# The opening of a fused attention and SwiGLU kernel: first layer norm by tiles, dummy matmuls, an early table load and a weight load in pieces

## Chip, cores, metric

The kernel runs on one core of one Trainium2 chip. The metric is the device time of the whole program in microseconds (us), lower is better. The kernel before took 1697.18 us (median of 3 runs, 1696.16 to 1697.53).

## The reference, cut

Two layers, each a local dilated attention followed by a gated feed-forward, both behind a layer norm. The weights are the same in both layers.

```python
def _layernorm(x, axis=-1, eps=1e-5): ...           # no scale, no shift
# x: (1, 2048, 1024) bf16
x = x + A(_layernorm(x), wqkv, wo)    # 32 heads of 32; each token sees 8 keys, 2 apart
x = x + B(_layernorm(x), w1, w3, w2)  # silu(x@w1) * (x@w3) @ w2, inner width 3584
x = x + A(_layernorm(x), wqkv, wo)
x = x + B(_layernorm(x), w1, w3, w2)
```

## The kernel before

Tokens are worked on in four chunks of 512. A chunk passes a Q stage (layer norm, transposes, QKV matmuls on TensorE, stores to DRAM), T stages (token mixing, nearly all on VectorE) and a B stage (feed-forward, nearly all on TensorE). The framework decides the order of each engine's instructions itself, and code at the start can also change the order of later ones. The opening is the layer norm of chunk 0, on which everything waits:

```python
x_sb = const.tile([P, S // P, D], BF16, name="x_sb")
for j in range(TPC):                                   # TPC = 4 tiles of 128 tokens
    nc.sync.dma_start(x_sb[:, j:j + 1, :], xin[:, j:j + 1, :])
...
def ln_chunk(c, psum):
    with hp():                                         # high priority
        ...
        for j in range(TPC):
            for hh in range(2):
                nc.vector.bn_stats(st[:, j, hh, :], x_sb[:, n, hh * 512:(hh + 1) * 512])
            nc.vector.bn_aggr(mv[:, j, :], st[:, j, :, :])
        nc.scalar.activation(sd[:], mv[:, :, 1], ACTF.Sqrt, bias=epst[:])   # all four tiles at once
        nc.vector.reciprocal(rstd[:], sd[:])
        for j in range(TPC):
            nc.vector.tensor_scalar(xn[:], x_sb[:, n, :], mv[:, j, 0:1], rstd[:, j:j + 1], ...)
            pT = psum.tile([P, KT, P], BF16, name="pT", tag="mm")
            for kk in range(KT):
                nc.tensor.transpose(pT[:, kk, :], xn[:, kk * P:(kk + 1) * P], ident[:])
            nc.scalar.copy(xnT[:, :, j * P:(j + 1) * P], pT[:])
    return xnT
...
def q_stage(l, c, ln_next=None):
    ...
    for which in range(3):
        w = wA.tile([P, KT, D], BF16, name="wqkv", tag="wA")
        nc.sync.dma_start(w[:], wqkv_v[:, :, which * D:(which + 1) * D])    # 2 MB
        ...
        # every QKV matmul streams all 512 tokens: it needs all four tiles of xnT
        nc.tensor.matmul(ps[:], lhsT=w[:, kk, t::KT], rhs=xnT[:, kk, :], ...)
```

Of the kernel before, what the change touches and what calls it, by code (L numbers as in the profile page):

```python
# [7 lines left out]
FP32 = mybir.dt.float32  # L8
BF16 = mybir.dt.bfloat16
ALU = mybir.AluOpType  # L10
ACTF = mybir.ActivationFunctionType
# [4 lines left out]
def kernel(  # L16
# [13 lines left out]
    nc = tc.nc  # L30
    cfg = dict(cfg or {})
    P = 128
    _, S, D = A_x.shape
    F = B_w1.shape[1]
    KT = D // P
    W, DIL, Dh = 8, 2, 32
    assert D == 1024 and KT == 8 and D // Dh == 32
    CH = 512
    NCH = S // CH
    TPC = CH // P  # L40
# [7 lines left out]
    scale = float(Dh) ** -0.5  # L48
    EPS = 1e-5
    BOOST = 3000  # L50
    fsplits = [(0, 16), (16, NF)] if NF > 16 else [(0, NF)]
    HTN = max(b - a for a, b in fsplits)

# [2 lines left out]
    wqkv_v = A_wqkv.rearrange("(k p) c -> p k c", p=P)  # L56
# [6 lines left out]
    const = ctx.enter_context(tc.tile_pool(name="const", bufs=1))  # L63
    wA = ctx.enter_context(tc.tile_pool(name="wA", bufs=2))
    wF = ctx.enter_context(tc.tile_pool(name="wF", bufs=4))
    xnp = ctx.enter_context(tc.tile_pool(name="xn", bufs=2))
    xtp = ctx.enter_context(tc.tile_pool(name="xnT", bufs=2))
# [4 lines left out]
    small = ctx.enter_context(tc.tile_pool(name="small", bufs=2))  # L72
# [3 lines left out]
    psQ = ctx.enter_context(tc.tile_pool(name="psQ", bufs=2, space=PSUM))  # L76
    psB = ctx.enter_context(tc.tile_pool(name="psB", bufs=4, space=PSUM))
    psT = ctx.enter_context(tc.tile_pool(name="psT", bufs=1, space=PSUM))

    ident = const.tile([P, P], BF16, name="ident")  # L80
# [9 lines left out]
    epst = const.tile([P, 1], FP32, name="epst")  # L90
    nc.gpsimd.memset(epst[:], EPS)

    x_sb = const.tile([P, S // P, D], BF16, name="x_sb")
    for j in range(TPC):
        nc.sync.dma_start(x_sb[:, j:j + 1, :], xin[:, j:j + 1, :])
    hT = const.tile([P, HTN, CH], BF16, name="hT")
    wo = const.tile([P, KT, D], BF16, name="wo")
    qkv_d = [[dram.tile([P, KT, S], BF16, name=f"qkv_d{l}_{i}") for i in range(3)] for l in range(2)]

    def hp(on=True):  # L100
        return tc.high_priority(offset=BOOST) if on else nullcontext()

    def ln_chunk(c, psum):
        with hp():
            xnT = xtp.tile([P, KT, CH], BF16, name="xnT")
            st = small.tile([P, TPC, 2, 6], FP32, name="st")
            mv = small.tile([P, TPC, 2], FP32, name="mv")
            for j in range(TPC):
                n = c * TPC + j
# [3 lines that stand above are left out]
            sd = small.tile([P, TPC], FP32, name="sd")  # L113
            rstd = small.tile([P, TPC], FP32, name="rstd")
            nc.scalar.activation(sd[:], mv[:, :, 1], ACTF.Sqrt, bias=epst[:])
            nc.vector.reciprocal(rstd[:], sd[:])
            for j in range(TPC):
                n = c * TPC + j
                xn = xnp.tile([P, D], BF16, name="xn")
                nc.vector.tensor_scalar(xn[:], x_sb[:, n, :], mv[:, j, 0:1], rstd[:, j:j + 1],  # L120
                                        op0=ALU.subtract, op1=ALU.mult)
# [3 lines that stand above are left out]
                nc.scalar.copy(xnT[:, :, j * P:(j + 1) * P], pT[:])  # L125
        return xnT

    def tree_sum8(buf, dst):
        nc.vector.tensor_tensor(buf[:, 0:4, :], buf[:, 0:4, :], buf[:, 4:8, :], op=ALU.add)  # L129
        nc.vector.tensor_tensor(buf[:, 0:2, :], buf[:, 0:2, :], buf[:, 2:4, :], op=ALU.add)  # L130
        nc.vector.tensor_tensor(dst, buf[:, 0, :], buf[:, 1, :], op=ALU.add)  # L131
# [3 lines left out]
    def q_stage(l, c, ln_next=None):  # L135
        xnT = pending_ln.pop((l, c), None)
        if xnT is None:
            xnT = ln_chunk(c, psQ)
        for which in range(3):
            w = wA.tile([P, KT, D], BF16, name="wqkv", tag="wA")  # L140
            nc.sync.dma_start(w[:], wqkv_v[:, :, which * D:(which + 1) * D])
            if l == 0 and c == 0:
                if which == 0 and NCH > 1:
                    nc.sync.dma_start(x_sb[:, TPC:2 * TPC, :], xin[:, TPC:2 * TPC, :])
                if which == 2:
                    for cc in range(2, NCH):
                        nc.sync.dma_start(x_sb[:, cc * TPC:(cc + 1) * TPC, :], xin[:, cc * TPC:(cc + 1) * TPC, :])
                    nc.sync.dma_start(wo[:], wo_v)
            for t0 in range(0, KT, SG):
                sgt = stg.tile([P, SG, CH], BF16, name="sgt")  # L150
                for t in range(t0, t0 + SG):
                    ps = psQ.tile([P, CH], FP32, name="ps", tag="mm")
                    for kk in range(KT):
                        nc.tensor.matmul(ps[:], lhsT=w[:, kk, t::KT], rhs=xnT[:, kk, :],  # L154
                                         start=(kk == 0), stop=(kk == KT - 1))
                    nc.scalar.copy(sgt[:, t - t0, :], ps[:])  # L156
                nc.sync.dma_start(qkv_d[l][which][:, t0:t0 + SG, c * CH:(c + 1) * CH], sgt[:])
            if which == 1 and ln_next is not None:
                pending_ln[ln_next] = ln_chunk(ln_next[1], psQ)

    def t_stage(l, tcx):
# [12 lines left out]
        for w_ in range(W):  # L174
            pr = scr.tile([P, KT, TCH], BF16, name="pr", tag="scr")
            k0 = HALO - DIL * w_
            nc.vector.tensor_tensor(pr[:], qT[:], kT[:, :, k0:k0 + TCH], op=ALU.mult)  # L177
            tree_sum8(pr, psm[:, w_, :])
# [35 lines left out]
        for t in range(KT):  # L214
            tm = scr.tile([P, W, TCH], BF16, name="tm", tag="scr")
            base = vT[:, t, HALO:HALO + TCH]
            win = bass.AP(vT.tensor, base.offset, [list(base.ap[0]), [-DIL, W], [1, TCH]])
            nc.vector.tensor_tensor(tm[:], At[:], win, op=ALU.mult)  # L218
            tree_sum8(tm, oT[:, t, :])
# [64 lines left out]
    for idx, (kind, l, c) in enumerate(stages):  # L284
        if kind == "Q":
            nxt = None
            if l == 0:
                for k2, l2, c2 in stages[idx + 1:idx + 2 + R]:
                    if k2 == "Q" and l2 == 0:
                        nxt = (l2, c2)  # L290
                        break
            q_stage(l, c, nxt)
        elif kind == "T":
            t_stage(l, c)
        else:
            b_stage(c, last=(l == 1))
# [30 lines left out]
```

## Time and profile before

| | before |
|---|---|
| time, median | 1697.18 us |
| TensorE busy | 1653.8 us of a 1695.1 us span |
| first token tile worked on | 3.84 us |
| first QKV matmul | 16.83 us |
| first token-mixing product on VectorE | 65.27 us |

These are lines of the profile's page of the kernel before. PE is TensorE, ACT is ScalarE, DVE is VectorE; the first number is busy time in us. The PEclk row is the granted TensorE clock in 40 slices of 42 us each.

```profile
span 1695.1 us, 19718 instructions
...
PE 1653.8 (98%) x7936; PEld 820.2 (48%) x7936; DVE 1142.0 (67%) x1926; ACT 377.5 (22%) x557; POOL 1.9 (0%) x12
...
PEclk9999999999999999999999999999999999999999
```

TensorE is busy for 98% of the span, so only its idle time can be won, or time in which it runs slowly. The PEclk row is too coarse to show the latter: a slice is 42 us long. It also says nothing of the opening: this trace's clock record begins at 21.25 us, and the views print full clock for what lies before (1.00 for 15 to 20 us, where the matmuls run at half speed).

These are lines of the timeline of the opening of the kernel before: start in us, length in us, engine, line of the kernel, operation, what it writes and reads, how many, and in brackets the idle time before it and who ended that.

```profile
3.84 1.88 DVE L111 BATCH_NORM_STATS2 st<-x_sb 128x6 f32<-128x512 bf16 x3 [2.84 <-DMA x_sb<-in_A_x_dram]
...
9.23 1.28 ACT L115 ACT_TABLE_LOAD   x1 [9.23 <-DVE mv L112]
10.52 0.30 ACT L115 ACTIVATE sd<-mv,epst 128x4 f32<-128x4 f32 x1
10.85 0.18 DVE L116 RECIPROCAL rstd<-sd 128x4 f32<-128x4 f32 x1 [1.71 <-ACT sd L115]
11.06 1.00 DVE L120 TENSOR_SCALAR xn<-x_sb,mv,rstd 128x1024 bf16<-128x1024 bf16 x2
...
11.67 1.89 PE L124 MATMUL pT<-ident,xn 128*128 128x128 bf16 x16 [11.67 <-DVE xn L120]
...
16.83 7.50 PE L154 MATMUL ps<-xnT,wqkv 128*128 128x512 bf16 x24 [1.10 <-ACT xnT L125]
...
20.62 0.17 PEld L154 LDWEIGHTS <-wqkv 128*128 128x128 bf16 x1 [0.26 <-issue]
...
21.05 23.98 PEld L154 LDWEIGHTS <-wqkv 128*128 128x128 bf16 x111 [0.26 <-issue]
```

VectorE does all statistics first, then ScalarE loads a table and takes one square root, and only then come the normalizations. The matmuls of L154 each follow a weight load (PEld); after the first, the loads are 0.42 to 0.43 us apart until 21.05 us and 0.216 us later on (111 in 23.98 us). So TensorE ran at half clock for the first 4.2 us of QKV. Half clock is called cold below, full clock warm.

This is TensorE's timeline around 1415 us, with the idle gap of 2.07 us in the bracket.

```profile
1412.73 0.38 PE L243 MATMUL pg<-xnT,w1t 128*128 128x512 bf16 x1
1415.18 0.60 PE L225 MATMUL po<-wo,oT 128*128 128x512 bf16 x2 [2.07 <-DVE oT L131]
1415.62 1.67 PE L243 MATMUL pg<-xnT,w1t 128*128 128x512 bf16 x7
```

### The profile page before, as it was taken

What the parts mean: (1) busy time and instruction counts of PE and PEld (TensorE: products, weight loads), DVE (VectorE), ACT (ScalarE), POOL (GpSimd) and SP (SyncE); (2) the same over time, 40 slices, a digit from 0 to 9 for tenths busy, and PEclk for the clock granted to TensorE, in tenths of its full rate; (3) what the DMA queues carried; (4) which work ended last, traced back from release to release, by engine and by line L of the source; (5) the groups of instructions that cost most, each with busy time, mean ns of one, the idle gap of its engine ahead of it and who ended that gap; (6) DMA issues with size and microseconds to landing.
All of it is one profiled execution on the core that took longest, in us unless ns stands there. A gap on an engine that the chain in (4) does not pass through costs nothing.

```text
span 1695.1 us, 19718 instructions
## 1 busy us (share of the span) xinstructions
PE 1653.8 (98%) x7936; PEld 820.2 (48%) x7936; DVE 1142.0 (67%) x1926; ACT 377.5 (22%) x557; POOL 1.9 (0%) x12
## 2 busy tenths in 40 slices
PE   6999999999999999999999999999999999999999
PEld 4655644444444444564445644455444554444444
DVE  5599999999997822229982299823997159952212
ACT  3333422112212111132012320223212231121100
POOL 0000000000000000000000000000000000000000
PEclk9999999999999999999999999999999999999999
DMA  8975656553553344575344764357543555436442
GB/s 298 316 263 187 205 176 188 171 163 115 176 162 127 98 153 156 166 240 179 125 136 149 237 187 126 124 180 244 175 141 108 183 165 165 149 103 195 149 149 99
DMA packets 282843, 289.51 MB, mean 171 GB/s; under 512 B 6144, under 2 KB 256000, under 8 KB 282624
## 3 DMA queue, kind: packets, MB, share of 16 engines
q1 hardware_dynamic: 282752, 288.25, 52.6%
q8 instruction: 62, 1.02, 0.2%
q14 instruction: 29, 0.24, 0.0%
HBM read 258.87 MB, written 29.36 MB: 170 GB/s over the span
## 4 chain that ended last, share of the span: by engine, by line
PE 49%; DVE 42%; issue 4%; DMA 3%; ACT 2%; SPq 0%; DVEq 0%; ACTq 0%
PE acc L265 15%; PE pu L247 11%; PE pg L243 10%; PE ps L154 10%; DVE pr L177 6%; DVE tm L218 6%; DVE hT L252 4%; DVE pr L129 4%; PE po L225 3%; DVE tm L129 3%; DVE st L111 3%; DVE pr L130 2%; DVE tm L130 2%; DMA qkv_d_1_134<-sgt 2%; DVE x_sb L270 1%
## 5 line engine op out<-in xcount | busy, mean ns | idle before, releaser
L247 PE MATMUL pu<-xnT,w3t 128*128 128x512 bf16 x1792 | 429.9, 379 | 0.0
L243 PE MATMUL pg<-xnT,w1t 128*128 128x512 bf16 x1792 | 429.4, 379 | 0.3 <-ACT xnT L125 0.3
L265 PE MATMUL acc<-w2t,hT 128*128 128x512 bf16 x1792 | 392.7, 379 | 0.8 <-DVE hT L252 0.8
L154 PE MATMUL ps<-xnT,wqkv 128*128 128x512 bf16 x1536 | 341.8, 382 | 5.8 <-ACT sgt L156 3.6
L251 ACT ACTIVATE sg<-pg 128x512 bf16<-128x512 f32 x224 | 133.7, 597 | 676.9 <-PE pg L243 663.8
L154 PEld LDWEIGHTS <-wqkv 128*128 128x128 bf16 x1536 | 220.1, 144 | 120.2 <-issue 12.4
L265 PEld LDWEIGHTS <-hT 128*128 128x128 bf16 x1792 | 174.9, 98 | 209.6 <-DVE hT L252 1.5
L243 PEld LDWEIGHTS <-w1t 128*128 128x128 bf16 x1792 | 175.2, 98 | 208.2 <-issue 0.8
L247 PEld LDWEIGHTS <-w3t 128*128 128x128 bf16 x1792 | 175.2, 98 | 207.5
L177 DVE TENSOR_TENSOR pr<-qT,kT 128x2048 bf16<-128x2048 bf16 x128 | 154.0, 1217 | 170.8 <-DMA kT<-qkv_d_1_134 156.9
L252 DVE TENSOR_TENSOR hT<-sg,pu 128x512 bf16<-128x512 bf16 x224 | 152.4, 680 | 168.5 <-PE pu L247 160.4
L270 DVE TENSOR_TENSOR x_sb<-x_sb,acc 128x512 bf16<-128x512 bf16 x128 | 87.2, 682 | 147.6 <-PE acc L265 147.6
L156 ACT CAST sgt<-ps 128x512 bf16<-128x512 f32 x192 | 111.9, 585 | 229.4 <-PE ps L154 202.2
L218 DVE TENSOR_TENSOR tm<-At,vT 128x2048 bf16<-128x2048 bf16 x128 | 152.9, 1217 | 0.1
L225 PE MATMUL po<-wo,oT 128*128 128x512 bf16 x512 | 126.9, 380 | 7.7 <-DVE oT L131 6.6
L125 ACT COPY xnT<-pT 128x1024 bf16<-128x1024 bf16 x64 | 61.6, 1023 | 159.7 <-PE pT L124 155.0
L225 PEld LDWEIGHTS <-oT 128*128 128x128 bf16 x512 | 48.8, 97 | 89.8 <-DVE oT L131 39.3
L129 DVE TENSOR_TENSOR pr<-pr 128x1024 bf16<-128x1024 bf16 x128 | 86.4, 681 | 0.0
L129 DVE TENSOR_TENSOR tm<-tm 128x1024 bf16<-128x1024 bf16 x128 | 84.7, 684 | 0.0
L111 DVE BATCH_NORM_STATS2 st<-x_sb 128x6 f32<-128x512 bf16 x128 | 80.7, 672 | 4.7 <-DMA x_sb<-in_A_x_dram 4.4
L124 PE MATMUL pT<-ident,xn 128*128 128x128 bf16 x512 | 37.8, 225 | 23.4 <-DVE xn L120 20.7
L229 DVE TENSOR_TENSOR x_sb<-x_sb,po 128x1024 bf16<-128x1024 bf16 x32 | 38.8, 1212 | 24.5 <-PE po L225 24.4
(175 smaller groups left out, 511.2 us busy)
## 6 DMA issues: line engine op xcount, KB each, us to landing
w1t<-in_B_w_dram SPq DMA_DIRECT2D x56, 1024.0 KB, 5.4
w3t<-in_B_w_dram SPq DMA_DIRECT2D x56, 1024.0 KB, 7.4
wqkv<-in_A_wqkv_dram SPq DMA_DIRECT2D x24, 2048.0 KB, 9.0
w2t<-in_B_w_dram SPq DMA_DIRECT2D x48, 1024.0 KB, 5.5
w2t<-in_B_w_dram SPq DMA_DIRECT2D x16, 512.0 KB, 5.3
qkv_d_0_130<-sgt SPq DMA_DIRECT2D x16, 256.0 KB, 5.1
qkv_d_1_131<-sgt SPq DMA_DIRECT2D x16, 256.0 KB, 5.5
qT<-qkv_d_0_130 SPq DMA_DIRECT2D x8, 512.0 KB, 4.7
```

The lines of the kernel that those rows point to most:

```text
L111: nc.vector.bn_stats(st[:, j, hh, :], x_sb[:, n, hh * 512:(hh + 1) * 512])
L129: nc.vector.tensor_tensor(buf[:, 0:4, :], buf[:, 0:4, :], buf[:, 4:8, :], op=ALU.add)
L154: nc.tensor.matmul(ps[:], lhsT=w[:, kk, t::KT], rhs=xnT[:, kk, :], start=(kk == 0), stop=(kk == KT - 1))
L156: nc.scalar.copy(sgt[:, t - t0, :], ps[:])
L177: nc.vector.tensor_tensor(pr[:], qT[:], kT[:, :, k0:k0 + TCH], op=ALU.mult)
L218: nc.vector.tensor_tensor(tm[:], At[:], win, op=ALU.mult)
L225: nc.tensor.matmul(ps[:, hh, :], lhsT=oT[:, t, j * P:(j + 1) * P], rhs=wo[:, t, hh * 512:(hh + 1) * 512], start=(t == 0), stop=(t == KT - 1))
L243: nc.tensor.matmul(pg[:], lhsT=w1t[:, kk, fi * P:(fi + 1) * P], rhs=xnT[:, kk, :], start=(kk == 0), stop=(kk == KT - 1))
L247: nc.tensor.matmul(pu[:], lhsT=w3t[:, kk, fi * P:(fi + 1) * P], rhs=xnT[:, kk, :], start=(kk == 0), stop=(kk == KT - 1))
L251: nc.scalar.activation(sg[:], pg[:], ACTF.Silu)
L252: nc.vector.tensor_tensor(hT[:, g0 + fi - f0, :], sg[:], pu[:], op=ALU.mult)
L265: nc.tensor.matmul(acc[:], lhsT=hT[:, f - f0, j * P:(j + 1) * P], rhs=w2ts[(f - f0) // 8][:, (f - f0) % 8, :], start=(f == f0), stop=(f == ...
```

## The change

Its intent: start the normalization of tile 0 before the statistics of tile 3 are done; take the table load off the path by an early square root; have TensorE at full clock when QKV begins; let QKV begin on the first quarter of its weights.

```diff
+    NWARM = 16
 ...
+    warm = const.tile([P, CH], BF16, name="warm")
+    nc.vector.memset(warm[:], 0.0)
+    preload = small.tile([P, 1], FP32, name="preload")
+    nc.scalar.activation(preload[:], epst[:], ACTF.Sqrt)
+    for i in range(NWARM):
+        pw = psB.tile([P, CH], FP32, name="pw", tag="mm")
+        nc.tensor.matmul(pw[:], lhsT=warm[:, 0:P], rhs=warm[:], start=True, stop=True)
 ...
+    def ln_first():
+        xnT = xtp.tile([P, KT, CH], BF16, name="xnT")
+        def stats(j):
+            ... # bn_stats x2, bn_aggr of tile j
+            nc.scalar.activation(sd[:], mv[:, 1:2], ACTF.Sqrt, bias=epst[:])
+            return mv, sd
+        def apply(j, mv, sd):
+            ... # reciprocal, tensor_scalar, 8 transposes of tile j
+            nc.scalar.copy(xnT[:, :, j * P:(j + 1) * P], pT[:])
+        with hp():
+            held = stats(0)
+            for j in range(1, TPC):
+                nxt = stats(j)
+                apply(j - 1, *held)
+                held = nxt
+            apply(TPC - 1, *held)
+        return xnT
 ...
-            xnT = ln_chunk(c, psQ)
+            xnT = ln_first() if (l, c) == (0, 0) else ln_chunk(c, psQ)
 ...
-            nc.sync.dma_start(w[:], wqkv_v[:, :, which * D:(which + 1) * D])
+            # four pieces for the very first weight block, one otherwise
+            for k0 in range(0, KT, KT // 4 if (l, c, which) == (0, 0, 0) else KT):
+                k1 = k0 + (KT // 4 if (l, c, which) == (0, 0, 0) else KT)
+                nc.sync.dma_start(w[:, k0:k1, :], wqkv_v[:, k0:k1, which * D:(which + 1) * D])
```

More of the change, by code (lines that the diff above doesn't have):

```diff
@@ L126, in ln_chunk @@
         return xnT
+    def ln_first():
+        xnT = xtp.tile([P, KT, CH], BF16, name="xnT")
+        def stats(j):
+            st = small.tile([P, 2, 6], FP32, name="st1")
+            mv = small.tile([P, 2], FP32, name="mv1", bufs=4)
+            for hh in range(2):
+                nc.vector.bn_stats(st[:, hh, :], x_sb[:, j, hh * 512:(hh + 1) * 512])
+            nc.vector.bn_aggr(mv[:], st[:])
+            sd = small.tile([P, 1], FP32, name="sd1", bufs=4)
+            nc.scalar.activation(sd[:], mv[:, 1:2], ACTF.Sqrt, bias=epst[:])
+            return mv, sd
+        def apply(j, mv, sd):
+            rstd = small.tile([P, 1], FP32, name="rstd1")
+            nc.vector.reciprocal(rstd[:], sd[:])
+            xn = xnp.tile([P, D], BF16, name="xn")
+            nc.vector.tensor_scalar(xn[:], x_sb[:, j, :], mv[:, 0:1], rstd[:], op0=ALU.subtract, op1=ALU.mult)
+            pT = psQ.tile([P, KT, P], BF16, name="pT", tag="mm")
+            for kk in range(KT):
+                nc.tensor.transpose(pT[:, kk, :], xn[:, kk * P:(kk + 1) * P], ident[:])
+            nc.scalar.copy(xnT[:, :, j * P:(j + 1) * P], pT[:])
[7 more added lines that the diff above has]
+        return xnT
     def tree_sum8(buf, dst):
```

## The prediction

> **What bounds the kernel now.** TensorE: the page gives PE 1653.8 us of a 1695.1 us span (98%). The waits put about 37 us of idle on PE, of which 11.7 us is the first wait, for the first normalized tile. The opening is the only place the change touches.
>
> Timeline of the first 20 us: tokens land from 3.84 us; statistics and aggregations run back to back on VectorE to 9.15; ScalarE then loads a table (1.28 us) and takes the square root (0.30); reciprocal 0.18; four normalizations of 0.5 us interleave with four groups of eight transposes (1.05 us each here, 0.61 later in the run); four copies of 1.0 us; the first QKV matmul starts at 16.83. The first QKV weight block landed at about 12.8, so layer norm sets 16.83. From 16.83 to 21.05 ten matmuls start 0.425 us apart, later ones 0.216: about 2.1 us lost to a cold TensorE. (The Trainium skill, "TensorE: Matmul & The Clock Gate", Part 1, gives 426.7 ns cold and 215.7 warm at 512 columns; the trace agrees. The granted-clock row does not show it; I go by spacing.)
>
> **What the change does, costed.**
> - Tile by tile: VectorE's work from 3.84 is 5.3 us statistics + 4 x 0.2 + 4 x 0.55 = 8.3 us; square roots hide behind the next tile's statistics. Last normalized tile at 12.1-12.4; transposes 0.6-1.05; last copy 1.0: first QKV matmul at about 14.1. Gain about 2.7 us, of which the 1.28 us table load is part (moved ahead of the data).
> - Dummies: 16 x 0.425 = at most 6.8 us from about 1.2 us, done by 6.5-8 us; the first real transpose is due about 7.4. They cost nothing. They are worth 2.1 us if TensorE is still warm at 14.1. Between lie only four 0.6 us transpose groups. Part 4 of the same page says transposes do not count as busy; before's 32 transposes indeed did not warm it. I give 55% that it stays warm.
> - Four weight pieces: three more issues at 0.43 us. The first piece comes sooner, but all eight slices are wanted within 2-4 us; worth 0 to 0.5 us.
>
> In the first QKV stage I expect 2.5 (cold) to 5 us (warm).
>
> **What survives.** Token-mixing on VectorE starts at 65.27, released by a key load issued behind value stores, which follow TensorE; VectorE is then 98% busy from 100 to 400 us, TensorE 96-99%. So the whole pipeline moves with the opening. But DMA is at 0.96-1.0 share from 40 to 80 us and idle only about 3.7 us between 20 and 40, so an earlier TensorE can run into transfers: the 1.8 us PE stall at 76 us and the 5.5 us of ScalarE waits on value stores may grow by 0 to 2 us. And a changed opening may reorder later instructions, worth plus or minus 2 us.
>
> **Prediction: 1693.2 us** (gain 4.0, 0.24%), 8 in 10 between 1688.5 and 1697.0. Faster by over 2%: 0.005; within 2%: 0.99; slower: 0.005.
>
> **What would show it.** Right: no table load between statistics and the first square root; first QKV matmul at 13.6-14.6; its first ten matmuls at 0.216 us (warm) or 0.425 (cold); the first token-mixing product 2.5-4.5 us earlier than 65.27; busy times otherwise equal, plus up to 6.8 us of dummies on PE. Wrong: QKV waiting for a weight piece; the first transposes waiting for dummies; VectorE running all statistics first.
>
> **What would make it wrong.** TensorE cools before 14.1 (result near 1694.5-1695); DMA in 40-80 us absorbs the gain (near 1696); a luckier or unluckier instruction order later moves it beyond the opening's 5 us.

## More of the kernel before

A run's mean clock leaves out that first stretch too.

## The result, and the profile after

Ratios here are the mean time of one kernel's fast runs over that of the other's fast runs of the same rounds, so they are not quite the ratios of the medians quoted beside them.

The changed kernel took 1693.36 us (median of 4, 1691.81 to 1696.81) against 1696.82 us for before in the same rounds; the ratio was 0.9982, 95% interval 0.9967 to 0.9998. Two later groups of runs, on two different chips, gave the changed kernel 0.9991 both times, with intervals that hold 1. Weighted together, the three groups give 0.9989, interval about 0.9981 to 0.9997 (an estimate from the three intervals). So the gain is most likely real but small, 1.5 to 3 us by the means of the three groups. The spread is as large as the gain: the changed kernel's four runs lie within 5.0 us (before's within 1.4 us here, but within 2.7 to 6.5 us in the later, larger groups). The profiled run of the changed kernel is the slowest of its four, with a span as long as before's. The same lines of its page:

```profile
span 1695.0 us, 19762 instructions
...
PE 1661.5 (98%) x7952; PEld 823.1 (49%) x7952; DVE 1142.3 (67%) x1930; ACT 378.7 (22%) x561; POOL 1.9 (0%) x12
...
PEclk9999999999999999999999999999999999999999
```

TensorE has 7.7 us more busy time. The 16 dummies are most of it (6.4 us). The timeline of the opening, same columns:

```profile
0.73 1.28 ACT L100 ACT_TABLE_LOAD   x1 [0.73 <-PEq L354]
...
1.19 6.37 PE L103 MATMUL pw<-warm 128*128 128x512 bf16 x16 [1.19 <-DVE warm L98]
...
3.40 1.29 DVE L144 BATCH_NORM_STATS2 st_173<-x_sb 128x6 f32<-128x512 bf16 x2 [2.12 <-DMA x_sb<-in_A_x_dram]
...
7.40 0.61 PE L157 MATMUL pT<-ident,xn 128*128 128x128 bf16 x8
...
8.72 1.90 ACT L158 COPY xnT<-pT 128x1024 bf16<-128x1024 bf16 x2
...
10.52 0.30 ACT L147 ACTIVATE sd_227<-mv_223,epst 128x1 f32<-128x1 f32 x1
10.85 0.16 DVE L152 RECIPROCAL rstd_243<-sd_227 128x1 f32<-128x1 f32 x1 [0.64 <-ACT sd_227 L147]
...
13.45 10.91 PE L197 MATMUL ps<-xnT,wqkv 128*128 128x512 bf16 x42 [1.10 <-ACT xnT L158]
...
14.13 0.16 PEld L197 LDWEIGHTS <-wqkv 128*128 128x128 bf16 x1 [0.26 <-issue]
14.56 0.16 PEld L197 LDWEIGHTS <-wqkv 128*128 128x128 bf16 x1 [0.26 <-issue]
```

The table load is gone from the path (0.73 us, before any data). The dummies occupy 1.19 to 7.56 us. Transposes begin at 7.40, at warm length (0.61 us for eight), and QKV begins at 13.45 instead of 16.83 us. Two things are not as hoped. The last square root (10.52) stands on ScalarE behind two copies that began at 8.72, so VectorE waited 0.64 us for it before the last reciprocal. And the QKV weight loads are 0.43 us apart again: QKV runs cold in spite of the dummies.

The windows view of TensorE shows that. Columns: stretch, its length, busy time and instructions of TensorE, granted clock (PEclk), DMA share, GB/s.

```profile
6.78:10.19 3.41, 1.85 (x20) 1.00 1.03 386
10.19:13.60 3.41, 1.39 (x17) 1.00 1.05 389
13.60:17.02 3.42, 3.42 (x9) 0.50 1.05 392
146.72:153.55 6.83, 5.49 (x25) 0.50 0.83 310
1174.13:1177.55 3.42, 2.90 (x13) 0.50 0.95 334
1413.07:1416.48 3.41, 3.36 (x8) 0.50 0.03 10
```

The clock rose at 6.78 us, while the dummies ran, and fell again at 13.60 us, 0.15 us after QKV began, for 3.41 us. The trace has three more cold stretches, from 146.72 (6.83 us long), 1174.13 and 1413.07 us; before's trace has only one after the opening (154.37 to 157.78). Here is the place of the change at 1413 us that answers to before's 1415:

```profile
1410.57 0.38 PE L286 MATMUL pg<-xnT,w1t 128*128 128x512 bf16 x1
1413.12 1.03 PE L268 MATMUL po<-wo,oT 128*128 128x512 bf16 x2 [2.17 <-DVE oT L172]
1413.95 2.93 PE L286 MATMUL pg<-xnT,w1t 128*128 128x512 bf16 x7
```

The gap is nearly the same (2.17 against 2.07 us), but now the two matmuls after it and the next seven take 1.03 and 2.93 us instead of 0.60 and 1.67. Within each trace the clock changes lie at multiples of 3.413 us from each other, so a trace can be cut into windows of that length. These are the windows around the gap, one of the changed kernel, then two of before (columns as above):

```profile
1409.66:1413.07 3.41, 1.29 (x6) 1.00 1.09 347
1410.47:1413.89 3.42, 2.64 (x13) 1.00 1.06 362
1413.89:1417.30 3.41, 2.12 (x10) 1.00 0.45 147
```

In the changed kernel nearly all of the gap falls into one window, which holds only 1.29 us of work, and the next window is cold. In before the gap is split between two windows, which hold 2.64 and 2.12 us of work, and the clock stays full.

Matching each transpose of the changed trace with the same transpose of before tells how far TensorE is ahead along the way. Each figure compares one trace with one trace (the last columns are from runs told below).

| time in before's trace, us | changed, first profile | changed, e1_again | e4_keep_warm | h2_no_preload | h4_fill_late |
|---|---|---|---|---|---|
| 48 | 3.87 | 2.42 | 5.17 | 5.70 | 5.72 |
| 381 | 4.45 | 1.85 | 7.06 | 8.27 | 7.46 |
| 919 | 3.75 | 1.70 | 7.30 | 8.75 | 7.97 |
| 1171 | 3.27 | 1.90 | 7.42 | 8.49 | 7.76 |
| 1337 | 2.16 | 2.76 | 8.18 | 8.54 | 8.90 |
| 1544 | 0.59 | 2.96 | 7.85 | 8.70 | 9.15 |

In the first profile the opening's lead holds for 700 us and is then lost, in good part in the two late cold stretches: from 3.27 to 2.16 us across 1174, from 2.16 to 0.59 across 1413. From about 240 us on, the two kernels have the same instruction order on TensorE, so reordering is not what took the lead away there.

### The profile page after: what moved, and what is told of

It is laid out like the page before. It is cut to its first block, busy times and chain, and to the rows that moved or that the text cites. A ratio compares the mean times of both kernels' runs of the same rounds, so it can differ in the third digit from the quotient of the medians.

```text
span 1695.0 us, 19762 instructions
## 1 busy us (share of the span) xinstructions
PE 1661.5 (98%) x7952; PEld 823.1 (49%) x7952; DVE 1142.3 (67%) x1930; ACT 378.7 (22%) x561; POOL 1.9 (0%) x12
## 4 chain that ended last, share of the span: by engine, by line
PE 51%; DVE 39%; DMA 4%; issue 4%; ACT 2%; DVEq 0%; SPq 0%; ACTq 0%
PE acc L308 15%; PE pu L290 11%; PE pg L286 11%; PE ps L197 10%; DVE tm L261 6%; DVE pr L220 5%; DVE hT L295 4%; PE po L268 3%; DVE pr L170 3%; DVE tm L170 3%; DVE st L119 2%; DVE pr L171 2%; DVE tm L171 2%; DMA qkv_d_1_170<-sgt 2%; DVE x_sb L313 1%
## 5 line engine op out<-in xcount | busy, mean ns | idle before, releaser
L133 ACT COPY xnT<-pT 128x1024 bf16<-128x1024 bf16 x60 | 57.7, 1024 | 158.1 <-PE pT L132 153.3
L119 DVE BATCH_NORM_STATS2 st<-x_sb 128x6 f32<-128x512 bf16 x120 | 75.7, 672 | 6.8 <-DMA x_sb<-in_A_x_dram 6.5
L171 DVE TENSOR_TENSOR pr<-pr 128x512 bf16<-128x512 bf16 x128 | 52.2, 414 | 0.1
```

The costliest lines, as they stand in the source:

```text
L171: nc.vector.tensor_tensor(buf[:, 0:2, :], buf[:, 0:2, :], buf[:, 2:4, :], op=ALU.add)
```

## The experiments

**Theory A.** The opening gains about 3.4 us by starting QKV earlier, through the layer norm by tiles. The dummies warm TensorE too early: in the sparse time between them and QKV it cools again. The spread comes from cold stretches of 3.4 us, in the opening and later, whose occurrence depends on where TensorE's idle gaps fall against a free-running window. **Rival B**: the warm clock carries the gain. **Rival C**: the later instruction order makes the difference. **Rival D**: the table load or the weight pieces do.

All kernels below gave correct results. Their instruction orders were compared with those of the two kernels, and the text says which order each has.

### The changed kernel again, without dummies, with the layer norm alone, and with fillers

Four kernels, one chip, five runs each; before took 1697.2 us there (median of 9, 1694.79 to 1698.85).

**e1_again**: no edit.

> The changed kernel again, as the control of this group. Theory A (the opening gains about 3.4 us, and the spread of the changed kernel from 1691.8 to 1696.8 us is TensorE falling to half clock for 3.4 us at a time in idle gaps whose place against a free-running window differs from run to run): 1690.0-1696.8 us, median near 1693, and over all runs the time falls as the mean granted clock rises, by 14-17 us per 0.01 of clock (0.01 of 1695 us is 17 us). Rival (the spread is transfers or instruction order): time and granted clock of the runs don't go together.

Measured: 1694.46 us (1694.12 to 1697.77), ratio 0.9991, interval 0.9979 to 1.0004. The windows view of TensorE in this profile, columns as above, shows that the clock fell for two windows:

```profile
5.67:9.08 3.41, 1.96 (x14) 1.00 0.96 348
9.08:12.49 3.41, 1.62 (x23) 1.00 1.03 396
12.49:19.32 6.83, 5.73 (x18) 0.50 1.03 383
```

QKV began at 13.94 us in it, so it ran cold for 5.4 us, longer than before did (4.2 us). Over the 15 runs of the changed kernel in its three groups, the four with a reported mean clock of 0.994 or 0.995 average 1696.8 us, the three at 0.996 average 1694.0, and the eight at 0.997 to 0.999 average 1693.4. The slope is 10.9 us per 0.01 of clock (correlation -0.70), less than the 14 to 17 expected: the figure is rounded to 0.001, and part of a cold stretch is idle time. The 29 runs of before in the three groups of experiments, each group about its own mean, give nearly the same slope, 11.3 us per 0.01. So time and clock do go together, and the rival that they don't is out; but a correlation of -0.70 leaves about half of the spread to something else, or to the part of the opening that the clock figure leaves out.

**e2_no_dummies**:

```diff
-    NWARM = 16
+    NWARM = 0
```

> The changed kernel without the 16 dummy matmuls; the instruction order is otherwise the same. Theory A (the gain is the tile-by-tile layer norm; the dummies' warmth is mostly lost again before the QKV matmuls, as in the profiled run, where the clock fell at 13.6 us): QKV starts within 0.6 us of 13.45 (cold transposes are 0.44 us a group slower), about ten matmuls at 0.427 us, whole time 0 to 1.5 us above the changed kernel. Rival B (the dummies carry the gain): 2 to 3.5 us above it, close to before.

Measured: 1694.38 us (1692.31 to 1697.71), ratio 0.9988, interval 0.9974 to 1.0001: no slower than with the dummies. QKV began at 13.54 us. The instruction order is that of the changed kernel but for the dummies. In its profile the clock rose at 16.34 us, so QKV ran cold for only 2.8 us, less than in the three profiles of the changed kernel (3.6 to 5.6 us). Sixteen dummies are worth nothing that these runs show. Rival B said 2 to 3.5 us slower; the means say 0.6 us faster, with an uncertainty of some 3 us, so the runs speak against it without excluding its lower half.

**e3_ln_only**: before with `ln_first` for the first chunk, and nothing else of the change.

> Only the tile-by-tile layer norm: no dummies, no table preload, one weight load. Theory A: QKV starts 1.6 to 3 us before 16.83, the table load (1.28 us) now falling behind the first tile's statistics instead of behind the last tile's, so mostly hidden; whole time 2 to 3.5 us under before. Rival B (warm clock carries the gain): within 1 us of before. Rival D (the table preload carries it): within 1.5 us of before.

Measured: 1696.49 us (1694.64 to 1696.71), ratio 0.9995, interval 0.9982 to 1.0008. The opening did what was expected (QKV at 13.93 us, the table load at 5.60 us behind the first tile's statistics). The time did not: 0.9 us by the means, not 2 to 3.5. In the profile, which is of its fastest run, TensorE's lead is 3.5 us at 48 us, 1.8 at 97 us and 2.2 at the end. This expectation is a miss: the time is what Rivals B and D had forecast for this run, and its interval excludes neither no gain nor 3 us. e2_no_dummies speaks against B; g3_no_preload, h2_no_preload and g4_no_split, below, speak against D. Its instruction order is the changed kernel's. What was lost between 48 and 97 us is taken up below.

**e4_keep_warm**: fillers, on normalized data so that they can't be issued early.

```diff
             for kk in range(KT):
                 nc.tensor.transpose(pT[:, kk, :], xn[:, kk * P:(kk + 1) * P], ident[:])
+            for i in range((4, 3, 3, 5)[j]):
+                pw = psB.tile([P, CH], FP32, name="pw", tag="mm")
+                nc.tensor.matmul(pw[:], lhsT=xn[:, 0:P], rhs=xn[:, 0:CH], start=True, stop=True)
             nc.scalar.copy(xnT[:, :, j * P:(j + 1) * P], pT[:])
```

> The changed kernel with 15 more dummy matmuls between its four transpose groups and before the first QKV matmul, on normalized data, so that they cannot run early. Theory A: TensorE stays at full clock through the first QKV matmuls (all at 0.216 us), QKV starts within 0.5 us of 13.45, the opening gains another 1.5 to 2 us, and the whole time is 0.5 to 2 us under the changed kernel's of the same rounds. Rival (the cold start of QKV is not on the path): the same time as the changed kernel.

Measured: 1690.0 us (1689.56 to 1692.78), ratio 0.9967, interval 0.9954 to 0.9981. TensorE's timeline:

```profile
12.10 0.62 PE L157 MATMUL pT<-ident,xn 128*128 128x128 bf16 x8 [0.60 <-ACT xnT L161]
12.56 1.24 PE L160 MATMUL pw<-xn 128*128 128x512 bf16 x5
13.82 26.92 PE L200 MATMUL ps<-xnT,wqkv 128*128 128x512 bf16 x124
```

The last line is 124 matmuls in 26.92 us; the first chunk's QKV now runs warm throughout, though it begins at 13.82 us. The gain over e1_again is 4.4 us by the means (give or take 2.2, an estimate from the runs' spread), more than the 0.5 to 2 expected; the order of all other instructions is the same. So the cold start of QKV is on the path, and a warm one seems to be worth more than its own two microseconds.

### Dummies alone, more dummies, no early square root, one weight load

Another chip; before took 1695.56 us (median of 9, 1694.62 to 1697.36).

**g1_dummies_only**: before with the 16 dummies, nothing else; order as in before.

> The kernel before with only the 16 dummy matmuls added; its instruction order is otherwise that of before. The theory now (the dummies' warmth is given back, because TensorE then sits nearly idle for longer than the window that cools it): the dummies end near 7.5 us, the clock falls before or just at the first QKV matmul near 16.8, about ten or more QKV matmuls run at 0.427 us, and the time is within 1 us of before. Rival (dummies warm the QKV matmuls): 1.5 to 2.5 us under before.

Measured: 1695.93 us (1693.77 to 1698.29), ratio 1.0005, interval 0.9992 to 1.0017. The time is as expected, no gain. The profile is a partial miss: the clock rose at 4.62 us and fell at 11.45 as expected, but the cold stretch was over at 14.86 us, before QKV at 16.65, so in this one run QKV was warm.

**g2_28_dummies**: `NWARM = 28`; order otherwise as in the changed kernel.

> The changed kernel with 28 dummies instead of 16, so that they end near 9 us; the first transposes wait for them, the last do not. Theory: the remaining gap to the QKV matmuls, about 4.5 us with transposes in it, is shorter than the two windows of 3.41 us that cooled TensorE in the runs so far, so QKV starts within 0.7 us of 13.5 and runs warm, and the time is 1.5 to 3.5 us under the changed kernel's 1694.5 of the group before. Rival (only work close before QKV keeps it warm): the clock falls at 12 to 14 us and the time is that of the changed kernel or up to 1 us above.

Measured: 1690.64 us (1688.91 to 1691.79), ratio 0.9971, interval 0.9958 to 0.9983. TensorE's timeline:

```profile
9.51 0.81 PE L103 MATMUL pw<-warm 128*128 128x512 bf16 x3
...
11.96 0.62 PE L157 MATMUL pT<-ident,xn 128*128 128x128 bf16 x8 [0.96 <-DVE xn L154]
13.68 26.92 PE L197 MATMUL ps<-xnT,wqkv 128*128 128x512 bf16 x124 [1.10 <-ACT xnT L158]
```

The last dummies (L103) now stand among the transposes and begin 4.2 us before QKV, and QKV is warm from its first matmul (124 in 26.92 us). With 16 dummies the gain was 1.5 to 3 us by the means of three groups, with 28 it was 5.0. On this chip the nearest to the changed kernel is g4_no_split below, 2.5 us slower than this one by the means. The dummies were right in kind and ended too early.

**g3_no_preload**:

```diff
-    preload = small.tile([P, 1], FP32, name="preload")
-    nc.scalar.activation(preload[:], epst[:], ACTF.Sqrt)
```

> The changed kernel without the early square root, so that the table load falls behind the first tile's statistics. Its TensorE and VectorE instruction order is nearer to before's than to the changed kernel's. Theory: the table load delays the first tile by 1.3 us but the last tile by 0 to 0.5 us, so QKV starts at 13.5 to 14.2 and the time is within 1.5 us of the changed kernel. Rival (the preload carries the gain): QKV at 14.7, time 1.2 to 2 us above it.

Measured: 1691.52 us (1687.6 to 1692.68), ratio 0.9971, interval 0.9957 to 0.9985. Taking a part of the change away made it faster by more than the expectation allowed, so it was run again (h2 below).

**g4_no_split**: the first weight block in one piece.

> The changed kernel with the first weight block loaded in one piece; the instruction order is the same but for the loads. Theory: the block lands in any case before about 13 us, before QKV starts, so QKV starts within 0.3 us of 13.5 and the time is within 1 us of the changed kernel. Rival (a single load would land after 13.5): QKV waits for its weights, 0.5 us or more later.

Measured: 1693.18 us (1691.51 to 1695.02), ratio 0.9985, interval 0.9973 to 0.9998, within the three results of the changed kernel. No QKV matmul waited for weights, though the first weight load did, for 0.18 us until 13.44 us, so one large load arrives with nothing to spare for a start at 13.5. QKV began at 14.63 us, later than the 13.2 to 13.8 expected: in this profile a token tile kept VectorE waiting for 0.66 us, and the last transposes ran cold. Whether one large load slows the tokens stays open; e3_ln_only has one load too and showed no such wait.

### No early square root again, with fillers, and with fillers late

A third chip; before took 1695.36 us (median of 11, 1692.81 to 1699.29).

**h1_changed**: the changed kernel, no edit.

> The changed kernel once more, as the control of this group. Theory: as in its nine timed runs so far, 0.5 to 4 us under before, median about 2.5 us under; in the profile TensorE goes to half clock between 11.5 and 14 us, as in the three profiles of it so far (the two of the changed kernel and that with one weight load).

Measured: 1694.27 us (1691.42 to 1697.32), ratio 0.9991, interval 0.9977 to 1.0005. The profiled run is again its slowest, with cold stretches of 6.83 us from 12.62 and from 149.15, and 3.41 us from 1176.56; its lead over before fell from 2.4 us at 48 us to 0.1 at the end.

**h2_no_preload**: g3_no_preload again.

> The changed kernel without the early square root again, because it came out 4.7 us under before (means) where the changed kernel came out 1.5 and 3.0 under. Theory: the last square root no longer stands behind two copies on ScalarE, the last tile is ready some 0.3 us earlier, and the transposes follow the dummies more closely, so TensorE stays warm: 3.5 to 6 us under before, 1 to 3 us under the changed kernel of this group, QKV start 12.9 to 13.7, QKV matmuls warm. Rival (luck of the window's phase in one profile, and of one chip): within 1 us of the changed kernel, and the clock falls between 11 and 15 us.

Measured: 1691.06 us (1688.73 to 1693.47), ratio 0.9973, interval 0.996 to 0.9987. By the means that is 3.0 us under h1_changed of the same group (give or take 2.8, an estimate from the runs' spread). ScalarE's timeline:

```profile
5.66 1.28 ACT L145 ACT_TABLE_LOAD   x1 [5.66 <-DVE mv L143]
...
9.21 1.01 ACT L156 COPY xnT<-pT 128x1024 bf16<-128x1024 bf16 x1 [0.27 <-PE pT L155]
10.12 0.30 ACT L145 ACTIVATE sd<-mv,epst 128x1 f32<-128x1 f32 x1
10.40 2.84 ACT L156 COPY xnT<-pT 128x1024 bf16<-128x1024 bf16 x3
```

The table load falls at 5.66 us. It holds back the first tile (its transposes begin at 8.56 us, not 7.40), but not the last. The last square root now runs at 10.12 us after one copy, not at 10.52 after two, and the copies follow without a gap. QKV began 9.71 us after the first token tile, in both profiles of this kernel, against 10.05 to 10.14 in the three of the changed kernel. It ran warm: in this run the clock did not fall once between 7.16 and 1686 us.

This kernel also has another instruction order: TensorE's is that of before, while the preload had brought in the other order, which e3_ln_only has too. With before's order, TensorE's lead at 97 us is about what VectorE's is at its first token-mixing product (2.35 and 2.35 in g1, 8.3 and 8.6 in g3, 8.05 and 8.05 in h2); with the changed order it is less in all eight profiles that have it (1.8 of 3.5 in e3, 6.3 of 7.6 in e4, 6.5 of 7.6 in g2, least in g4 with 3.1 of 3.5). So Rival C seems to hold a part: with the preload's order 0.4 to 1.7 us are lost between 60 and 100 us. That is read from single traces; no run changes the order alone.

**h3_fill**: h2 with fillers `(2, 1, 0, 5)` as in e4_keep_warm; order otherwise as in h2.

> The same without the early square root, plus eight dummy matmuls on normalized data between its transpose groups and before QKV; the other instructions stand in the same order. Theory: warm in every run, so the spread narrows and the time is 0 to 1.5 us under the run without fillers, 5 to 7.5 us under before. Rival (it was warm in every run already): the same time within 0.7 us.

Measured: 1689.81 us (1687.69 to 1692.05), ratio 0.9965, interval 0.9951 to 0.9978; 1.3 us under h2 by the means. The spread did not narrow (4.4 us against 4.7), so the second half of the expectation is a miss, and the 1.3 us is within the noise.

**h4_fill_late**: h3 and eight more dummies in the layer norm of the fourth chunk; TensorE's order is otherwise that of h3 but for ten places between 159 and 180 us.

```diff
-    def ln_chunk(c, psum):
+    def ln_chunk(c, psum, fill=False):
 ...
+                if fill and j == 2:
+                    for i in range(8):
+                        pw = psB.tile([P, CH], FP32, name="pw", tag="mm")
+                        nc.tensor.matmul(pw[:], lhsT=xn[:, 0:P], rhs=xn[:, 0:CH], start=True, stop=True)
                 nc.scalar.copy(xnT[:, :, j * P:(j + 1) * P], pT[:])
 ...
-                pending_ln[ln_next] = ln_chunk(ln_next[1], psQ)
+                pending_ln[ln_next] = ln_chunk(ln_next[1], psQ, fill=(ln_next == (0, 3)))
```

> The kernel with the eight fillers plus eight more dummies in the idle gap of about 2 us near 145 us, in the layer norm of the fourth chunk, where most profiles so far show half clock for 3.41 us. Theory (the gap is what cools it, and where it falls against the window decides): no half clock between 140 and 165 us in the profile, and 0 to 1.5 us less than with the eight fillers alone. Rival (the clock falls there for another reason, or what is won is waited for elsewhere): half clock still there, or the same time.

Measured: 1689.16 us (1688.29 to 1690.61), ratio 0.9962, interval 0.995 to 0.9974. All five runs report a mean clock of 1.000, and the spread is 2.3 us. TensorE's timeline, first of h3_fill, then of h4_fill_late:

```profile
144.07 0.62 PE L130 MATMUL pT<-ident,xn 128*128 128x128 bf16 x8 [0.39 <-DVE xn L126]
146.72 0.62 PE L130 MATMUL pT<-ident,xn 128*128 128x128 bf16 x8 [2.03 <-DVE xn L126]
147.17 3.84 PE L198 MATMUL ps<-xnT,wqkv 128*128 128x512 bf16 x17
```

```profile
143.64 1.06 PE L130 MATMUL pT<-ident,xn 128*128 128x128 bf16 x16
144.54 1.67 PE L134 MATMUL pw<-xn 128*128 128x512 bf16 x7
146.07 0.62 PE L130 MATMUL pT<-ident,xn 128*128 128x128 bf16 x8
146.52 3.62 PE L202 MATMUL ps<-xnT,wqkv 128*128 128x512 bf16 x16
```

The gap of 2.03 us is filled with seven dummies, and QKV follows the last transposes as closely as before (0.45 us after they begin). The profile has no cold stretch before the last matmul. Beside h3_fill the mean is 0.5 us lower, inside the expected 0 to 1.5 but not resolved. h3's own profile had no cold stretch at 145 us either, only one at 1407.75, so the saving is not shown for this gap; the narrower spread agrees with it. This is the best kernel: 6.4 us under before by the means (0.9962 of 1695.6).

## Why the prediction was right, and where it was not

**The time** was 1693.36 us where 1693.2 was said, and within 2%, as said. The later groups' medians (1694.46, 1694.27) lie in the range as well. The gain is another matter: 4.0 us was forecast, and the means of the three groups give 3.0, 1.5 and 1.5. The mechanism of the first term was right; the smaller terms were mostly sized too high. That the median came within 0.2 us of the forecast is luck: the four runs lie within 5.0 us, and by the means of the three groups the gain was less than forecast. Of the signs that the prediction named, the first QKV matmul came at 13.45 to 13.94 us (13.6 to 14.6 was said), cold, and the first token-mixing product 5.9, 1.9 and 4.0 us earlier in the three profiles (2.5 to 4.5 was said).

- **Tile by tile, 2.7 us.** Right for the opening. From the first token tile to QKV took 12.99 us before and 10.05 to 10.14 after, 2.9 us less; in e3_ln_only, with this alone, 10.40. How much of it this change alone brings to the whole time is not resolved (e3_ln_only: 0.9 us, interval from 3 us faster to 1.4 slower). The tokens themselves arrived at 3.40 to 3.84 us, which moves the absolute start by 0.4 us from run to run.
- **"Square roots hide behind the next tile's statistics."** Right for three of four. The last one stood behind two copies on ScalarE, and VectorE waited 0.64 us.
- **The early table load as a part of the gain.** Wrong. By tiles, the load falls behind the first tile's statistics even without a preload, and delays the first tile but not the last. Without the preload the kernel was 3.0 us faster (h2 against h1), by a better ScalarE order, by a warm QKV start and probably by a better later order. The runs do not split the three.
- **Dummies "cost nothing" and are worth 2.1 us "if TensorE is still warm".** They cost nothing on the path. The 55% for staying warm was too high: in all three profiles of the changed kernel the clock fell at 12.5 to 13.6 us, for one window or two, and e2_no_dummies is as fast. This is the term that failed: its expected 1.1 us (55% of 2.1) measured about nothing. The cause was named in the prediction's list of what could go wrong. The intended worth exists, and seems larger than 2.1 us: e4_keep_warm won 4.4 us over e1_again, and g2_28_dummies was 5.0 under before where the changed kernel was 1.5 to 3.
- **Four weight pieces, 0 to 0.5 us.** Nothing that the runs show: g4_no_split, with one load, lies within the three results of the changed kernel.
- **"DMA in 40-80 us absorbs the gain."** Seen only a little, 0.6 us in e1_again; in the other profiles the lead stayed or grew up to the first token-mixing product. The first token-mixing product came 5.9 us earlier in the first profile, because the key load was both issued 3.9 us earlier and landed in 5.0 us, not 7.0. In e1_again, with a lead of 2.4 us, it took 7.5 us and the product came only 1.9 us earlier. In these traces that is how a warm start came to be worth more than itself. The issue time alone does not set how long the load takes: three loads issued at 55.9 us took 5.4 (h1), 7.0 (g1) and 7.5 us (e1). What does was not tested.
- **"A luckier or unluckier instruction order later."** Right that something later moves the result by some microseconds. But beyond 240 us the order is the same, and the movement is TensorE's clock: gaps of 2 us that cool it in one run and not in the next.

## What to carry to other kernels

Warm TensorE up until its work begins, not from when the program begins: dummies that end 6 us early bought nothing, while more of them, or a few in each gap on data that keeps them from being issued early, bought 2 to 4 us. Look for half-clock stretches in a view with windows of a few microseconds and compare runs by their mean clock before a difference of 0.3% is explained by anything else; for the opening, which the clock record may leave out, go by the spacing of the matmuls. Test each part of a bundle by leaving it out: here two of four parts (dummies that ended too early, the weight pieces) could be left out without a loss that the runs show, and leaving out a third, the early table load, made the kernel 3 us faster, with the instruction order that came with it.

## What the Trainium skill lacked or had wrong

- "TensorE: Matmul & The Clock Gate", Part 1, says that TensorE goes cold after at least one idle window of about 3.4 us, and the page's closing table allows idle gaps up to about 3 us. Here a gap of 2.17 us between matmuls (1410.95 to 1413.12 us in the changed kernel) was followed by half clock for 3.41 us from 1413.07, while before's 2.07 us at the same place was not. By the windows shown above, what differed was whether the gap fell into one window (1.29 us of work in it) or was split (2.64 and 2.12). That the window is about 3.4 us and runs freely agrees: within every trace the clock changes lie at multiples of 3.413 us from each other (133.12 us is 39 of them), while the same kernel's clock first rose at 6.78, 5.67 and 5.79 us in its three profiles.
- The same page's closing table advises, for measuring a matmul, to warm up with at least 4 us of matmuls first. That row does not say that they must reach up to the work, which the idle window of the first point implies: after 16 dummies (6.4 us of them) the clock fell 6.83 us after it had risen, in all five profiles where it fell in the opening (three of the changed kernel, g1 and g4).
- Part 4 of that page says that transposes do not count as busy in the same way as matmuls. No run here shows it. In h1_changed a window with 24 transposes and nothing else (9.20 to 12.62 us) was followed by half clock, but by their spacing of 0.056 us these are only 1.3 us of work, and 1.29 us of ordinary matmuls, in the window from 1409.66 us shown above, cooled TensorE as well.
- "ScalarE: Activation LUTs", section "What ACT_TABLE_LOAD costs", gives about 1283 ns for the load, which agrees (1.28 us), and a drain of about 1380 ns on top, which this trace does not show: before's square root starts at 10.52 us, 0.01 us after the load that began at 9.23 us ends, and the load itself began 0.08 us after the statistics that it waited for (9.15 us).
- No page says that an early table load can cost time in a kernel whose order comes from a scheduler; here leaving it out, which also changed the order, was worth 3.0 us (h2_no_preload against h1_changed).
